# A two-layer decode kernel on one core: 1/std moved into the queries, output copies moved to ScalarE, the last weight loads cut differently

## The chip, the core and the metric

The kernel runs on one core of one Trainium2 chip. The metric is the device time of one execution in microseconds, given as the median of several runs. The core's engines run side by side, each in the order of its own instruction list: TensorE (PE, matmuls; PEld is its weight load), VectorE (DVE), ScalarE (ACT), GpSimd (POOL) and SyncE (SP, which here only issues transfers). Sixteen DMA engines bring data from the chip's memory; one `dma_start` is spread over all sixteen.

## The reference, cut to what matters

Four sequences (B = 4) are decoded by one token each. Width D = 640, 32 heads of DH = 128, a window of W = 1024 cached positions, FF = 1728. All is f32.

```python
x = A_x
for _ in range(2):
    n = layernorm(x)                          # (x - mean) / sqrt(var + 1e-5)
    q = n @ wq                                # per head: 4 x 128
    s = q . k[last 1024] * 128 ** -0.5        # per batch and head: 1024 scores
    x = x + (softmax(s) . v[last 1024]) @ wo
    x = x + relu(layernorm(x) @ w1) @ w2
```

Both rounds use the same weights and caches, so everything but what stays in the chip's SBUF is read twice.

## The kernel before, in words

**Data.** For each head the host packs one record of 128 rows x 9472 numbers (4736 KB): the head's columns of wq (`WQ`, 5 blocks of 128), keys (`K`, two halves of 4 batches x 512 positions), values (`V`, two halves) and its rows of wo (`WO`, 4 x 160). Records go in turn into five slots (`NS`) and a sixth, smaller buffer called `ring`. The last five heads of round 0 stay in their slots and are the first of round 1; head 26 (`SIXTH`) stays partly in `ring` and is next. w1 (5 blocks) and w2 (54 tiles of 128 x 160) of round 0 pass through `ring` in pieces (`MLP_RING`). In round 1, w1 goes into `ring`, w2 into one slot, cut into loads by `W2_SLOT`.

**Order of the loads.** `items` is the list of all loads, in order. `pump` issues the next load from SP as soon as no live data stands in its place; `done` says that a piece has been used and pumps again. A load also waits, on SP, until the semaphore that it is to count on is free. So one queue carries everything, in order, and what makes room for it is mostly TensorE's progress.

**Order of the work.** Each engine is wrapped in `InOrder`: what stands first in the code runs first on that engine. One turn of the loop over heads (line 442) puts down, for TensorE: the next head's scores, this head's values, the query of the head after the next (the first work on a newly landed record), `output_T` and `project`. VectorE in the same turn: `softmax`'s maximum (and its product with 1/std, line 347), `picks` (four operations), the copy of the new query into `qT` (line 329), the copy of the output into `oTs` (line 379), `weights` (seven operations). ScalarE: the exponential with its row sum.

**1/std.** `center` subtracts the mean from x, transposed in `xT`, and puts its squares' sums into `squares`; the division by the standard deviation is put off. `deviation` sums the squares over the partitions with a matmul into `o_ps[:, 8:12]`, one column for each batch, picks each partition's own batch with a mask (`of_batch` in attention, `pick` in the MLP; two VectorE operations), and takes the root on ScalarE into `rstd`, one number for each partition. `softmax` inverts it once per round and multiplies each head's maximum by it and, as the exponential's `scale`, the scores. In the MLP the ReLU takes it as its `scale`.

**The end.** After the last head, `center`, `mlp(1)`: 20 matmuls on w1 (the profile counts two for each f32 matmul), ReLU, two transposes, then 54 tiles of w2 in the order of their loads, adding into `acc`; VectorE copies `acc` and SP writes it out. `busy` is a matmul whose result nobody reads.

Of the kernel before, what the change touches and what calls it, by code (L numbers as in the profile page):

```python
# [32 lines left out]
F32 = mybir.dt.float32  # L33
AF = mybir.ActivationFunctionType
OP = mybir.AluOpType
AX = mybir.AxisListType
PSUM = bass.MemoryType.PSUM

P = 128
B, D, H, DH, W, FF = 4, 640, 32, 128, 1024, 1728  # L40
# [25 lines left out]

SIXTH_PIECES = [(3520, 5088), (5088, HELD), (0, 1600), (1600, 3520)]
W1_SLOT = [[0, 1], [2], [3], [4]]
W2_SLOT = [22, 20, 8, 4]
LATE = 5  # L70


# [22 lines left out]
def decode_kernel(ctx: ExitStack, tc: tile.TileContext, xf, rec, w1, w2, out):  # L95
    nc = tc.nc
    pe, dve, act, pool, sp = (InOrder(tc, e) for e in (nc.tensor, nc.vector, nc.scalar, nc.gpsimd, nc.sync))
    sb = ctx.enter_context(tc.tile_pool(name="sb", bufs=1))
# [11 lines left out]
    oTs = sb.tile([P, LATE, B], F32, name="oTs")  # L110
    qT = sb.tile([P, B], F32, name="qT")
    of_batch = sb.tile([P, B], F32, name="of_batch")
    of_block = sb.tile([P, 4], F32, name="of_block")
    pick = sb.tile([P, B], F32, name="pick")
    mrt = sb.tile([P, B], F32, name="mrt")
    small = sb.tile([P, 16], F32, name="small")
    nmax, rtot, rstd, eps, eps_dh, ones, unused, sums, tot0, tot1 = (small[:, i:i + 1] for i in range(10))
    squares, wq_mean, minus = small[:, 10:14], small[:, 14:15], small[:, 15:]
    tot = [tot0, tot1]
# [3 lines left out]
    sc_ps = [ps.tile([P, W], F32, name=f"sc_ps{i}") for i in range(2)]  # L123
    t_ps = ps.tile([P, 512], F32, name="t_ps")
    o_ps = ps.tile([P, 512], F32, name="o_ps")
# [33 lines left out]
    def home(h, r):  # L159

        if h == SIXTH:
            return "ring"
        return h % NS if not r or h >= LAST else (h + LAST) % NS
# [7 lines left out]
    def load(key, src, lo, hi, buf, col):  # L171
        items.append((key, src, lo, hi, buf, col))
# [14 lines left out]
    hs = order[0]  # L187
# [24 lines left out]
    n = 0  # L212
    for size in W2_SLOT:
        load(("w2", 1), w2, n * FD, (n + size) * FD, home(new[-5], 1), n * FD)
# [17 lines left out]
    def cols(key, lo, n):  # L232

        for x, y, buf, col in pieces(key):
            if x <= lo and lo + n <= y:
                return buffers[buf][:, col + lo - x:col + lo - x + n]
        raise KeyError((key, lo, n))
# [10 lines left out]
    def done(key, lo, hi):  # L248

        if key[0] == "rec" and key[1] == 0 and key[2] >= LAST:  # L250
            return
        if key == ("rec", 0, SIXTH):
            hi = min(hi, HELD)
        for x, y, buf, col in pieces(key):
            a, b = col + max(lo, x) - x, col + min(hi, y) - x
            if a < b:
                free(buf, a, b)
        pump()
# [18 lines left out]
    def busy(n, to=sc_ps[1]):  # L277

        pe.matmul(to[0:1, :n], ones, slot[home(LAST, 0)][:, K:K + n], start=True, stop=True)
# [30 lines left out]
        dve.tensor_tensor(spread[:, :KB * B].rearrange("p (k b) -> p k b", b=B), blocks, blocks, op=OP.mult)  # L310
        dve.tensor_reduce(squares, spread[:, :KB * B].rearrange("p (k b) -> p b k", b=B), op=OP.add, axis=AX.X)

    def deviation(rows, bias, scale):

        pe.matmul(o_ps[:, 8:8 + B], ones.to_broadcast([P, P]), squares, start=True, stop=True)
        dve.tensor_tensor(mrt, o_ps[:, 8:8 + B], rows, op=OP.mult)
        dve.tensor_reduce(sums, mrt, op=OP.add, axis=AX.X)
        act.activation(rstd, sums, AF.Sqrt, bias=bias, scale=scale / D)

    def xblock(k):  # L320
        return xT[:, 32 * k:32 * k + B]

    def query(r, h, s):
        q = sc_ps[s][:, :B]
        key = ("rec", r, h)
        for k in range(KB):
            pe.matmul(q, cols(key, WQ + k * DH, DH), xblock(k), start=(k == 0), stop=(k == KB - 1))
        done(key, WQ, K)
        dve.tensor_copy(qT, q)

    def scores(r, h, s, first=False):
        key = ("rec", r, h)
        for i in range(2):
            for b in range(B):
                pe.matmul(sc_ps[s][32 * b:32 * b + 4, 512 * i:512 * i + 512], qT[:, b:b + 1].to_broadcast([P, 4]),
                          cols(key, K + 512 * (B * i + b), 512), start=True, stop=True)
            done(key, K + VH * i, K + VH * i + VH)
            if first and i == 0:
                deviation(of_batch, eps_dh, float(DH))
                act.activation(unused, eps, AF.Exp)  # L340

    def softmax(s, first=False):

        dve.tensor_reduce(nmax, sc_ps[s], op=OP.max, axis=AX.X, negate=True)
        if first:
            dve.reciprocal(rstd, rstd)
        dve.tensor_tensor(nmax, nmax, rstd, op=OP.mult)
        act.activation(sc_ps[s], sc_ps[s], AF.Exp, bias=nmax, scale=rstd, accum_out=tot[s])

    def weights(s, parts=(0, 1)):  # L350
        if 0 in parts:
# [24 lines left out]

    def output_T(i, last=False):
        pe.matmul(o_ps[:, :B], on[last], pick, start=True, stop=True)
        dve.tensor_copy(oTs[:, i], o_ps[:, :B])

    def project(r, h, i, end):
        key = ("rec", r, h)
# [5 lines left out]
    def mlp(r):  # L388


        h_ps, front, back = sc_ps[0][:, :512], t_ps[:, :224], sc_ps[0][:, 512:768]
        for k in range(KB):
            for j in range(NB):
                pe.matmul(h_ps[32 * j:32 * j + B, :FQ], xblock(k), cols(("w1", r), k * FF + FQ * j, FQ),
                          start=(k == 0), stop=(k == KB - 1))
            done(("w1", r), k * FF, k * FF + FF)
            if k == 0:
                deviation(pick, eps, 1.0)
                dve.reciprocal(rstd, rstd)
            elif r == 0 and k < KB - 1:  # L400
                busy(512)
        act.activation(front, h_ps[:, :224], AF.Relu, scale=rstd)
        act.activation(back[:, :208], h_ps[:, 224:FQ], AF.Relu, scale=rstd)
        act.activation(back[:, 240:], h_ps[:, 416:FQ], AF.Relu, scale=rstd)
        dve.transpose(scratch[:, :224], front)
        dve.transpose(scratch[:, 224:], back)
        if r == 0:
            wq_means(LAST)
        else:
            busy(512)  # L410
        busy(256)
        key = ("w2", r)
        sizes = W2_SLOT if r else [size for name, size, _ in MLP_RING if name == "w2"]
        first = 0
        for i, size in enumerate(sizes):
            for s in range(first, first + size):
                m, n = TILES[s]
                w = cols(key, s * FD, FD)
                for part, q in ((m, n),) if m < 13 else ((13, n), (14, n + 2)):
                    pe.matmul(acc[32 * q:32 * q + B, :FD], hT[:, part, :B], w,  # L420
                              start=False, stop=(s >= len(TILES) - NB), skip_group_check=True)
            if r == 0 and i < len(sizes) - 2:
                busy(512)
            done(key, first * FD, (first + size) * FD)
            first += size
# [4 lines left out]
    for r in range(2):  # L430
        hs = order[r]
        late = LATE if r == 0 else 2
        if r == 0:
            center(fill=False)
            query(r, hs[0], 0)
        else:
            center(("rec", r, hs[0]))
        scores(r, hs[0], 0, True)
        softmax(0, True)
        query(r, hs[1], 1)  # L440
        weights(0)
        for n, h in enumerate(hs[:-2]):
            i = n - (H - late)
            s = (n + 1) % 2
            scores(r, hs[n + 1], s)
            softmax(s)
            values(r, h)
            picks(0)
            if n == H - 3:
                for _ in range(2):  # L450
                    busy(512)
            query(r, hs[n + 2], n % 2)
            output_T(max(i, 0))
            if i < 0:
                project(r, h, 0, False)
            weights(s, (0, 1) if n < H - 3 else (0,))
            if r == 0 and h == SIXTH:
                put_by()
            if r == 1 and hs[n + 2] == SIXTH:
                put_back()  # L460
        scores(r, hs[-1], 1)
        softmax(1)
        busy(512, sc_ps[0])
        weights(0, (1,))
        values(r, hs[-2], 0, (0, 1))
        weights(1)
        picks(0)
        values(r, hs[-1], 1, (1, 0))
        picks(1)
        dve.memset(sc_ps[0][:, 720:752], 0.0)  # L470
        output_T(late - 2)
        for i in range(late - 3):
            project(r, hs[H - late + i], i, False)
        if late == 2:
            project(r, hs[-2], 0, False)
        output_T(late - 1, True)
        for i in (late - 3, late - 1, late - 2) if late > 2 else (1,):
            project(r, hs[H - late + i], i, i == late - 2 or late == 2)
        center()
        mlp(r)  # L480
    dve.tensor_copy(x_sb, acc[:, :FD])
    sp.dma_start(out, x_sb)
# [38 lines left out]
```

## Time and profile before

| | |
|---|---|
| time, median of 3 runs | 714.68 us (714.43 to 715.10) |
| the profiled execution: its own time | 714.49 us |
| the profiled execution: span from first to last instruction | 712.8 us |
| granted TensorE clock, mean | 0.791 |
| busy: PE, DVE, ACT | 525.9 us (74%), 359.2 us (50%), 93.0 us (13%) |
| read from memory | 302.44 MB, 424 GB/s over the span |
| queue of the kernel's loads (q1) | 15264 packets, 99.1% of 16 engines' span |

The table is read from below: busy shares of the computing engines are means over the whole span, while the queue of the loads is at work nearly all of it. The queues q8 and q14 of the profile are the fetching of the engines' own instructions, by the same DMA engines. "Idle before" in a list of instructions is the time that an engine stood still just before one, with what ended it.

### The profile page before, as it was taken

The page shows a single profiled execution, that of the slowest core. Times are in us where ns is not written, and L with a number is a line of the kernel's source. Part 1 is how long each engine was busy: PE and PEld are TensorE (multiplying, and loading weights), DVE is VectorE, ACT ScalarE, POOL GpSimd, SP SyncE. Part 2 cuts the span into 40 slices and gives each one's busy share as a digit, 9 for nine tenths or more (in the row PEclk, how much of TensorE's full clock was granted, in tenths as well). Part 3 has the DMA queues.
Part 4 walks back from the last instruction along what each step waited for, and adds up shares of the span by engine and source line. Part 5 has one row for each costly group of instructions (what it writes and reads, how often), then busy time and mean ns, then how long its engine had stood idle before and what let it go on. Part 6 is the DMA issues. An engine that isn't in the chain of part 4 may idle for free.

```text
span 712.8 us, 8976 instructions
## 1 busy us (share of the span) xinstructions
PE 525.9 (74%) x3704; PEld 211.6 (30%) x3704; DVE 359.2 (50%) x1016; ACT 93.0 (13%) x145; POOL 1.1 (0%) x9
## 2 busy tenths in 40 slices
PE   4466877667676867778888898886777668777887
PEld 2132332313223232322324333332232323323323
DVE  3345445454444545445741787754644445445751
ACT  1201011010101011011111211201101010110201
POOL 0000000000000000000000000000000000000000
PEclk9987578786877676676999899877767775766997
DMA  9999999999999999999999999999999999999996
GB/s 375 442 435 428 427 439 437 428 426 442 435 422 434 439 435 421 432 441 420 425 412 395 427 434 428 445 427 436 433 436 428 435 432 430 432 437 420 430 423 287
DMA packets 15336, 303.10 MB, mean 425 GB/s; under 512 B 1712, under 2 KB 2112, under 8 KB 5312
## 3 DMA queue, kind: packets, MB, share of 16 engines
q1 hardware_dynamic: 15264, 302.52, 99.1%
q8 instruction: 29, 0.48, 0.2%
q14 instruction: 11, 0.09, 0.0%
q10 hardware_dynamic: 32, 0.01, 0.0%
HBM read 302.44 MB, written 0.08 MB: 424 GB/s over the span
## 4 chain that ended last, share of the span: by engine, by line
DMA 81%; PE 13%; DVE 4%; issue 1%; ACT 0%; another core or an unknown queue 0%; SPq 0%; DVEq 0%
DMA slot<-rec 69%; PE sc_ps L87 7%; DMA ring<-rec 6%; PE o_ps L87 3%; DMA ring<-w 3%; DMA slot<-w 3%; PE acc L87 3%; DVE scratch L87 2%; DVE small L87 1%; DVE oTs L87 1%; DVE t_ps L87 0%; ACT sc_ps L87 0%; DVE ring L87 0%; DVE mrt L87 0%
## 5 line engine op out<-in xcount | busy, mean ns | idle before, releaser
L87 PE MATMUL sc_ps<-xT,slot 128*128 128x4 f32 x620 | 100.5, 289 | 138.9 <-DMA slot<-rec 138.1
L87 PE MATMUL sc_ps<-slot,qT 128*4 128x512 f32 x992 | 195.0, 925 | 1.3 <-DVE qT L87 1.2
L87 PEld LDWEIGHTS sc_ps<-xT,slot 128*128 128x128 f32 x620 | 96.3, 240 | 194.4 <-issue 180.5
L87 ACT ACTIVATE sc_ps<-sc_ps,small 128x1024 f32<-128x1024 f32 (+1 forms) x68 | 76.6, 1127 | 551.1 <-DVE small L87 541.5
L87 PE MATMUL o_ps<-slot,scratch 128*16 128x512 f32 x960 | 137.1, 688 | 2.4 <-DVE scratch L87 1.8
L87 DVE TENSOR_REDUCE small<-sc_ps 128x1 f32<-128x1024 f32 x64 | 78.3, 1223 | 75.6 <-PE sc_ps L87 75.6
L87 DVE STREAM_TRANSPOSE t_ps<-sc_ps 128x512 f32<-128x512 f32 x128 | 93.2, 728 | 2.1
L87 DVE COPY qT<-sc_ps 128x4 f32<-128x4 f32 x63 | 10.1, 160 | 155.5 <-PE sc_ps L87 155.5
L87 PEld LDWEIGHTS o_ps<-slot,scratch 128*16 128x16 f32 x960 | 33.3, 121 | 131.4 <-issue 82.6
L87 DVE SCALAR_TENSOR_TENSOR scratch<-o_ps,of_block,scratch 128x128 f32<-128x128 f32 x186 | 65.2, 351 | 6.6
L87 PEld LDWEIGHTS sc_ps<-slot,qT 128*4 128x4 f32 x992 | 32.5, 113 | 80.2 <-issue 69.5
L87 PE MATMUL acc<-slot,oTs 128*4 128x160 f32 x496 | 36.8, 382 | 16.3 <-DVE oTs L87 15.8
L87 DVE TENSOR_SCALAR scratch<-o_ps,of_block 128x128 f32<-128x128 f32 x62 | 21.7, 350 | 37.2 <-PE o_ps L87 37.2
L87 PE MATMUL o_ps<-pick,scratch 128*128 128x4 f32 x128 | 29.4, 300 | 6.3 <-DVE scratch L87 6.1
L87 DVE TENSOR_TENSOR scratch<-t_ps,mrt 128x64 f32<-128x64 f32 x128 | 28.8, 225 | 4.7
L87 PEld LDWEIGHTS o_ps<-pick,scratch 128*128 128x128 f32 x128 | 26.2, 253 | 9.7 <-DVE scratch L87 8.9
L87 PE MATMUL sc_ps<-slot,small 128*1 128x512 f32 (+1 forms) x44 | 22.1, 599 | 2.9 <-DMA slot<-rec 2.4
L87 DVE COPY oTs<-o_ps 128x4 f32<-128x4 f32 x64 | 10.4, 162 | 15.5 <-PE o_ps L87 14.1
L87 DVE TENSOR_SCALAR mrt<-of_batch,small 128x4 f32<-128x4 f32 x64 | 14.7, 230 | 2.2
L87 DVE STREAM_TRANSPOSE scratch<-small 128x32 f32<-128x32 f32 x64 | 12.9, 202 | 2.4 <-ACT sc_ps L87 2.4
L87 PEld LDWEIGHTS acc<-slot,oTs 128*4 128x4 f32 x496 | 6.8, 84 | 22.1 <-DVE oTs L87 21.0
L87 PE MATMUL sc_ps<-ring,xT 128*4 128x432 f32 x80 | 10.3, 622 | 2.9 <-DMA ring<-w 2.6
(64 smaller groups left out, 118.5 us busy)
## 6 DMA issues: line engine op xcount, KB each, us to landing
slot<-rec SPq DMA_DIRECT2D x43, 4736.0 KB, 30.6
slot<-rec SPq DMA_DIRECT2D x17, 2368.0 KB, 17.1
slot<-rec SPq DMA_DIRECT2D x2, 4416.0 KB, 34.8
slot<-rec SPq DMA_DIRECT2D x7, 1024.0 KB, 9.0
ring<-w SPq DMA_DIRECT2D x8, 864.0 KB, 27.1
ring<-rec SPq DMA_DIRECT2D x1, 4576.0 KB, 40.1
slot<-rec SPq DMA_DIRECT2D x2, 2048.0 KB, 38.4
slot<-rec SPq DMA_DIRECT2D x3, 1344.0 KB
```

The source lines that it names most:

```text
L87: r = build(*args, **kwargs)
```

## The change

- `deviation` no longer picks each partition's batch before the root. The root of all four columns goes into a new tile `rstds` (128 x 4, each partition holds all four batches). The new function `row_rstd` inverts `rstds` and only then picks each partition's own number into `rstd` (three VectorE operations).
- `query` multiplies by `rstds` while it copies from PSUM to `qT`. The first head of each round is the exception: its query is copied (round 0) or corrected (round 1, in `center`) before 1/std is known, so its `softmax` does as before: `row_rstd`, the product of the maximum, `scale=rstd`. All other heads' `softmax` loses the product, and its exponential has `scale=1.0`.
- `output_T` copies the output with ScalarE (`AF.Copy`) instead of VectorE.
- The MLP calls `deviation` and `row_rstd(pick)`.
- `W2_SLOT`, the loads of w2 in round 1, becomes 22, 14, 10, 4 and 4 tiles instead of 22, 20, 8 and 4.

```diff
-W2_SLOT = [22, 20, 8, 4]
+W2_SLOT = [22, 14, 10, 4, 4]
...
+    rstds = sb.tile([P, B], F32, name="rstds")
...
-    def deviation(rows, bias, scale):
+    def deviation(bias, scale):
 
         pe.matmul(o_ps[:, 8:8 + B], ones.to_broadcast([P, P]), squares, start=True, stop=True)
-        dve.tensor_tensor(mrt, o_ps[:, 8:8 + B], rows, op=OP.mult)
-        dve.tensor_reduce(sums, mrt, op=OP.add, axis=AX.X)
-        act.activation(rstd, sums, AF.Sqrt, bias=bias, scale=scale / D)
+        act.activation(rstds, o_ps[:, 8:8 + B], AF.Sqrt, bias=bias, scale=scale / D)
+
+    def row_rstd(rows):
+
+        dve.reciprocal(rstds, rstds)
+        dve.tensor_tensor(mrt, rstds, rows, op=OP.mult)
+        dve.tensor_reduce(rstd, mrt, op=OP.add, axis=AX.X)
...
-    def query(r, h, s):
+    def query(r, h, s, first=False):
...
-        dve.tensor_copy(qT, q)
+        if first:
+            dve.tensor_copy(qT, q)
+        else:
+            dve.tensor_tensor(qT, q, rstds, op=OP.mult)
...
-                deviation(of_batch, eps_dh, float(DH))
+                deviation(eps_dh, float(DH))
...
         if first:
-            dve.reciprocal(rstd, rstd)
-        dve.tensor_tensor(nmax, nmax, rstd, op=OP.mult)
-        act.activation(sc_ps[s], sc_ps[s], AF.Exp, bias=nmax, scale=rstd, accum_out=tot[s])
+            row_rstd(of_batch)
+            dve.tensor_tensor(nmax, nmax, rstd, op=OP.mult)
+        act.activation(sc_ps[s], sc_ps[s], AF.Exp, bias=nmax, scale=rstd if first else 1.0, accum_out=tot[s])
...
-        dve.tensor_copy(oTs[:, i], o_ps[:, :B])
+        act.activation(oTs[:, i], o_ps[:, :B], AF.Copy)
...
-                deviation(pick, eps, 1.0)
-                dve.reciprocal(rstd, rstd)
+                deviation(eps, 1.0)
+                row_rstd(pick)
...
-            query(r, hs[0], 0)
+            query(r, hs[0], 0, True)
```

## The prediction, made before the changed kernel was run

> **What bounds the kernel now.** I read the page's DMA queues first, because they alone are near full.
>
> ```profile
> q1 hardware_dynamic: 15264, 302.52, 99.1%
> q8 instruction: 29, 0.48, 0.2%
> q14 instruction: 11, 0.09, 0.0%
> ```
>
> The columns are packets, MB and the share of 16 engines' span. The loads take 99.1%, and the change moves not a byte more or less. So only three things can move the end: what the slowest of the 16 DMA engines does beside the loads, gaps in the queue, and what follows the last landing. The chain of waits in order of time shows the landings (start us, length us, what):
>
> ```profile
> 197.92 30.86 DMA slot<-rec
> ...
> 232.63 30.74 DMA slot<-rec
> ...
> 510.25 31.24 DMA slot<-rec
> ...
> 545.34 30.54 DMA slot<-rec
> ...
> 578.26 31.12 DMA slot<-rec
> ...
> 613.13 29.75 DMA slot<-rec
> ...
> 683.10 23.86 DMA slot<-w
> 707.01 2.84 PE acc L87 x68
> ```
>
> Start plus length is a landing, complete only when the last of the 16 engines is done: 541.49, 575.88, 609.38, 642.88. Between them lie three records each, and the steps are 34.39, 33.50 and 33.50 us. The earlier pair, 228.78 and 263.37, is 34.59 apart. So some steps are 0.89 to 1.09 us too long. What stands in the long ones and not in the others? The DMA queues by narrow windows, in order at 43 to 44, 236.5 to 237, 559.1 to 559.8, 621.8 to 622.4 and 655.8 to 656.4 us, hold one small instruction packet each (11 packets of 0.09 MB in all: about 8 KB each):
>
> ```profile
> q14 instruction: 1, 0.01, 1.9%
> ...
> q14 instruction: 1, 0.01, 3.9%
> ...
> q14 instruction: 1, 0.01, 2.8%
> ...
> q14 instruction: 1, 0.01, 3.2%
> ...
> q14 instruction: 1, 0.01, 3.2%
> ```
>
> Eight of the eleven, of which the first, the third, the seventh and the last are shown here (all but the one at 622), come at a fixed count of VectorE instructions, as the busy table by stretches shows (x counts them):
>
> ```profile
> 0.00:43.30 43.30, 15.45 (x46) 0.96 0.97 413
> 43.30:655.80 612.50, 315.56 (x886) 0.77 1.00 430
> 655.80:712.80 57.00, 28.15 (x85) 0.86 0.90 383
> ```
>
> From the first fetch to the eighth are seven intervals, 886/7 = 126.6 instructions each. I read: VectorE's own instruction list is fetched in pieces, and the DMA engine that fetches it loses about a microsecond of its loads each time. That engine is then the last, and every landing waits for it. The end shows one engine alone (busy table, last columns DMA share and GB/s; then timelines of PE and PEld):
>
> ```profile
> 708.00:708.50 0.50, 0.50 (x20) 0.36 (x12) 0.00 (x0) 0.00 (x0) 0.00 (x0) 1.00 0.12 46
> 708.50:709.00 0.50, 0.50 (x22) 0.44 (x16) 0.00 (x0) 0.00 (x0) 0.00 (x0) 1.00 0.06 26
> ```
>
> ```profile
> 704.78 1.90 PE L87 MATMUL acc<-slot,scratch 128*4 128x160 f32 x44
> ```
>
> ```profile
> 708.56 0.45 PEld L87 LDWEIGHTS acc<-slot,scratch 128*4 128x4 f32 x16
> 709.35 0.11 PEld L87 LDWEIGHTS acc<-slot,scratch 128*4 128x4 f32 x8 [0.34 <-DMA slot<-w]
> ```
>
> A share of 0.06 is one engine of 16; 0.12 is two, or one and part of others. TensorE starts on the last four tiles at 709.35, released by the last load, and all that follows hangs on that.
>
> **The change part by part.** Costs are rows of the groups by form (count | busy us, mean ns):
>
> ```profile
> L87 DVE TENSOR_TENSOR small<-small 128x1 f32<-128x1 f32 x64 | 10.2, 159 | 2.2
> L87 DVE COPY oTs<-o_ps 128x4 f32<-128x4 f32 x64 | 10.4, 162 | 15.5 <-PE o_ps L87 14.1
> L87 DVE COPY qT<-sc_ps 128x4 f32<-128x4 f32 x63 | 10.1, 160 | 155.5 <-PE sc_ps L87 155.5
> L87 DVE TENSOR_TENSOR qT<-sc_ps,mrt 128x4 f32<-128x4 f32 x1 | 0.2, 161 | 0.2 <-PE sc_ps L87 0.2
> L87 ACT ACTIVATION_READ_ACCUMULATOR sc_ps<-sc_ps,small 128x1 f32 x64 | 12.2, 191 | 0.0
> L87 ACT ACTIVATE small<-small 128x1 f32<-128x1 f32 x6 | 1.6, 264 | 26.2 <-DVE small L87 26.2
> L87 DVE TENSOR_TENSOR mrt<-o_ps,of_batch 128x4 f32<-128x4 f32 x2 | 0.3, 163 | 3.5 <-PE o_ps L87 3.5
> L87 ACT ACTIVATE t_ps<-sc_ps,small 128x224 f32<-128x224 f32 x2 | 0.8, 422 | 8.0 <-PE sc_ps L87 8.0
> ```
>
> *Product in the query's copy.* The copy at 160 ns becomes a product at 161: nothing. *No product with the maximum* for 62 of 64 heads: 0.16 us less before each exponential. *Copies to ScalarE*: 64 x 0.162 us leave VectorE, with their wait for TensorE. No row has ScalarE copying four columns; the nearest lie at 0.191 and 0.264, and I take 0.25 (an ACTIVATE's, not the read-out's), so each copy is 0.03 to 0.10 us slower. In the turns where VectorE is never idle long this still shortens a head by up to 0.16 + 0.16 us and the wait; but the queue of the loads is full there, so it buys no time. Without that cover it would be worth some 0.5 us a head.
>
> *The end of round 1.* VectorE's copy stands behind `picks`, though TensorE has delivered long before:
>
> ```profile
> 692.25 0.39 PE L87 MATMUL o_ps<-pick,scratch 128*128 128x4 f32 x2
> ...
> 693.99 0.15 DVE L87 COPY oTs<-o_ps 128x4 f32<-128x4 f32 x1
> ...
> 695.01 0.16 DVE L87 COPY oTs<-o_ps 128x4 f32<-128x4 f32 x1 [0.86 <-PE o_ps L87]
> ...
> 696.01 0.33 DVE L87 TENSOR_REDUCE small<-acc 128x1 f32<-128x160 f32 x1 [0.84 <-PE acc L87]
> ```
>
> ScalarE can copy at about 692.7. The projection at 694.2 then goes ahead of the last `picks`, and the second copy, `center` (696.01) and ReLU come some 0.5 us earlier. The landing at 709.35 hides this too.
>
> *Root before the pick.* Two small VectorE operations (0.163 the row, the other alike) leave the path before the root and come back behind it; for the two first heads they now lie between maximum and exponential: +0.35 us, with gaps. Round 0's first is covered by the second record's landing. Round 1's is covered only by a full queue. In the MLPs ReLU waits for w1's matmuls (8.0 us idle, all ended by TensorE), not for this.
>
> *The loads of w2.* From 708.56 to 709.35 is 0.79 us for 4 tiles, from 707.01 to 708.56 1.55 us for 8: cutting costs 2 x 0.79 - 1.55 = 0.03 us a piece. Splitting helps TensorE start earlier, but TensorE already waits for the last piece. Ahead of it, TensorE's own work would not bind soon: 44 matmuls take 1.90 us, of which about 0.3 us is the last one's length (707.01 to 709.85 likewise ends one such length after its last start), so 0.037 each, and the 112 of all 54 tiles (two of them split) 4.5 us. Without waiting they would end at 709.3 from 704.78, at 708.8 with ReLU 0.5 us earlier, against 709.8 now.
>
> *The instruction lists.* VectorE loses 62 products and 64 copies: 46 + 886 + 85 = 1017 become 891 (the MLP and first-head parts cancel). Fetches stand at 46 + 126.6 k. For k = 6 that is 806, for k = 7 932, which is never reached: seven fetches, not eight. The slowest engine gets 0.89 to 1.09 us back. But the landing then falls to the next engine: one alone from somewhere in 708.0 to 708.5 until 709.0 is worth 0.5 to 0.75; I take 0.55, since 46 GB/s in the first half microsecond is nearly two engines' work (26 GB/s is one's).
>
> The sum: -0.55 + 0.03 = -0.52 us. The profiled execution took 714.49, its span 712.8; the median is 714.68, 0.19 above it. So the span becomes 712.3 and the median 714.16: **714.2 us**.
>
> **Rivals.**
>
> *Fetching costs nothing, or another engine fetches (0.26).* Then the full queue stays as it is: +0.03, **714.7**. For it: a step of 33.50 us (609.38 to 642.88) holds a q14 packet too, at 622 us, without being longer; I count that one to ScalarE's list, which another DMA engine may serve. Against it: the two long steps. The Trainium skill ("Runtime: NRT & Kernel Launch", section Instruction fetch mechanics) speaks for this rival: an engine fetches its list in blocks by its own DMA queue, and the cost of a block is "mostly hidden". By that rule the time stays at 714.7; the 34.39 us step of this trace says that on a full queue it does not hide.
>
> *More comes back (0.13).* The stretch of round 0's MLP is the one place where loads wait for room (busy table, DMA share and GB/s last; the third row is the full queue again):
>
> ```profile
> 372.00:376.00 4.00, 3.34 (x24) 0.42 (x19) 0.00 (x0) 0.00 (x0) 0.00 (x0) 1.00 0.95 360
> 384.00:388.00 4.00, 3.11 (x53) 1.65 (x45) 0.56 (x2) 0.00 (x0) 0.00 (x0) 1.00 1.01 367
> 392.00:396.00 4.00, 2.51 (x26) 0.84 (x29) 2.48 (x10) 1.96 (x4) 0.00 (x0) 1.00 1.02 426
> ```
>
> Against 426 GB/s these lose 4 x (1 - 360/426) = 0.62 and 0.55 us. An earlier slowest engine there frees pieces earlier; with half of the 1.17 and 0.9 instead of 0.55 the time is 714.68 - 0.9 - 0.58 + 0.03 = **713.2**. Against it: nothing in the change touches this stretch's matmuls.
>
> *Round 1 starts later (0.06).* The 0.35 us of the first exponential and 0.1 us for each copy of some eight heads delay the freeing of slots by up to 1.15 us. It decides only if the queue runs short after 388 us; the row at 392 says it does not. Price 0.35 to 1.15: **715.1 to 715.9**.
>
> *The fifth load of w2 ends by itself (0.05), the slower side.* The page lists a load that has the queue to itself:
>
> ```profile
> out<-scratch SPq DMA_DIRECT2D x1, 80.0 KB, 1.6
> ```
>
> That is 1.6 us from issue to landing for 80 KB, nearly all fixed. If the fifth load, which needs one more free semaphore, is issued only when the queue is empty, it costs 1.6 us at the very end: 714.68 + 1.6 = **716.3**. It decides if the issue comes after about 707 us; against it, the loads of w2 have their slot early: the chain has the second of them issued at 683.10. The Trainium skill ("DMA: Bandwidth & Descriptors", Anatomy of one DMA) gives a fixed 2.0 us for each DMA; were it paid in line, the sum would be 716.7. The 0.79 us between two landings says that it overlaps.
>
> **How the numbers follow.** Forecast 0.50, rivals 0.26, 0.13, 0.06, 0.05. A measurement of this kernel tells 0.2%, 1.43 us, from no change: 713.25 to 716.11. Of the "more" case nearly all lies below, with 0.02 from the forecast's edge: faster 0.15. The fifth-load case lies above: slower 0.05. The rest is within: 0.80. The range from 713.1 to 715.2 holds the forecast, the first rival, most of the second and the cheap end of the third.
>
> **What would show it.** In the new profile: about 891 VectorE instructions and one q14 packet fewer (or the same number, if ScalarE's longer list takes one more); steps of 33.5 us between landings except where VectorE's fetch falls, and three such fetches after 390 us instead of four; a last wait of TensorE for w2 near 708.8; `center` of round 1 near 695.5; SP issuing the fifth load before 700. I am wrong if the long steps stay where no fetch is, if the last landing is still at 709.3 with seven fetches, or if round 1's stretch after 388 us shows a DMA share under 1.

## The result, and the profile after

The changed kernel took **719.82 us** (median of 6 runs, 719.50 to 720.39) beside 715.31 us for the kernel before on the same chip. The ratio is **1.006**, 95% interval 1.0045 to 1.0075: slower by 0.6%, where 714.2 us was forecast with a range of 713.1 to 715.2. The profiled execution spans 717.7 us instead of 712.8.

The page's DMA queues after (packets, MB, share of 16 engines' span):

```profile
q1 hardware_dynamic: 15408, 302.52, 98.9%
q8 instruction: 29, 0.48, 0.3%
q14 instruction: 11, 0.09, 0.0%
```

The bytes are the same 302.52 MB, the 144 packets more are the fifth load of w2, and the queue is as full as before: 98.9% of a longer span. The queue did the same work in more time. The packets on q14 are eleven as before, not ten.

The chain of waits after (start us, length us, what):

```profile
119.52 31.61 DMA slot<-rec
...
153.52 31.30 DMA slot<-rec
...
187.20 31.30 DMA slot<-rec
...
222.37 29.81 DMA slot<-rec
...
492.22 30.33 DMA slot<-rec
...
526.41 29.82 DMA slot<-rec
...
696.51 17.78 DMA slot<-w
714.29 0.04 issue
714.34 0.50 PE acc L87 x8
```

Start plus length is a landing: 151.13, 184.82, 218.50 and 252.18, and later 522.55 and 556.23. Three records lie between neighbours, and each of these steps is 33.68 or 33.69 us. Before, the short steps were 33.50. So the loss isn't at one place: early and late in the run alike, a step is 0.18 us longer. The last load lands at 714.29, TensorE follows at once, and the end is as it was.

The busy table by stretches after (PE, PEld, DVE, ACT, POOL busy us with counts, then granted clock, DMA share, GB/s), cut at the first and the eighth fetch of VectorE, then round 1's start and the last half microseconds:

```profile
0.00:50.20 50.20, 25.43 (x130) 11.44 (x130) 17.20 (x48) 6.92 (x11) 1.13 (x9) 0.93 0.97 412
50.20:701.20 651.00, 487.19 (x3452) 194.52 (x3452) 321.54 (x839) 90.50 (x195) 0.00 (x0) 0.79 1.00 428
701.20:717.70 16.50, 7.45 (x132) 3.13 (x124) 1.19 (x3) 1.08 (x3) 0.00 (x0) 0.97 0.60 242
388.00:392.00 4.00, 3.18 (x44) 1.85 (x32) 1.40 (x7) 0.00 (x0) 0.00 (x0) 1.00 1.00 406
392.00:396.00 4.00, 4.00 (x24) 2.39 (x20) 1.76 (x5) 1.75 (x3) 0.00 (x0) 0.56 1.02 413
713.00:713.50 0.50, 0.50 (x20) 0.27 (x8) 0.00 (x0) 0.00 (x0) 0.00 (x0) 1.00 0.07 26
```

VectorE has 48 + 839 + 3 = 890 instructions, one from the 891 forecast. Yet an eighth fetch of its list came, with three of them left; the DMA queues at 701 to 701.6 us hold it:

```profile
q14 instruction: 1, 0.01, 3.4%
```

Round 1's start (the rows from 388 and 392 us) has a DMA share of 1.00 and 1.02, so the queue did not run short there. At 713.0 one DMA engine alone is still at work (0.07 of 16), as in the profile before.

The rows of the edits themselves, from the groups by form:

```profile
L87 ACT ACTIVATE sc_ps<-sc_ps,small 128x1024 f32<-128x1024 f32 x64 | 69.8, 1091 | 315.8 <-DVE small L87 315.8
L87 ACT ACTIVATE oTs<-o_ps 128x4 f32<-128x4 f32 x64 | 11.1, 174 | 246.0 <-PE o_ps L87 246.0
L87 DVE TENSOR_TENSOR qT<-sc_ps,rstds 128x4 f32<-128x4 f32 x62 | 9.9, 160 | 150.1 <-PE sc_ps L87 150.1
```

None of them has become dear, and the landings are what came later. So the lost time is looked for in the loads.

### The profile page after: what moved, and what is told of

Same layout as the page of the kernel before. It is cut to its first block, busy times and chain, and to the rows that moved or that the text cites. A ratio compares the mean times of both kernels' runs of the same rounds, so it can differ in the third digit from the quotient of the medians.

```text
span 717.7 us, 8921 instructions
## 1 busy us (share of the span) xinstructions
PE 520.1 (72%) x3704; PEld 209.1 (29%) x3704; DVE 339.9 (47%) x890; ACT 98.5 (14%) x209; POOL 1.1 (0%) x9
## 3 DMA queue, kind: packets, MB, share of 16 engines
q1 hardware_dynamic: 15408, 302.52, 98.9%
## 4 chain that ended last, share of the span: by engine, by line
DMA 73%; PE 21%; DVE 4%; ACT 1%; issue 1%; ACTq 0%; DVEq 0%
DMA slot<-rec 67%; PE sc_ps L87 12%; PE o_ps L87 6%; DMA ring<-w 3%; DVE scratch L87 3%; PE acc L87 3%; DMA slot<-w 2%; ACT oTs L87 1%; ACT sc_ps L87 0%; DVE small L87 0%; DVE t_ps L87 0%; ACTq L87 0%; ACT t_ps L87 0%; DVE xT L87 0%; DVE qT L87 0%
## 5 line engine op out<-in xcount | busy, mean ns | idle before, releaser
L87 PE MATMUL sc_ps<-slot,qT 128*4 128x512 f32 x992 | 198.5, 942 | 1.0 <-DVE qT L87 1.0
L87 PEld LDWEIGHTS sc_ps<-xT,slot 128*128 128x128 f32 x620 | 94.6, 236 | 201.1 <-DMA slot<-rec 183.7
L87 PE MATMUL o_ps<-slot,scratch 128*16 128x512 f32 x960 | 131.5, 665 | 0.9 <-DVE scratch L87 0.9
L87 ACT ACTIVATE sc_ps<-sc_ps,small 128x1024 f32<-128x1024 f32 (+1 forms) x68 | 71.1, 1046 | 315.9 <-DVE small L87 315.8
L87 DVE TENSOR_TENSOR qT<-sc_ps,rstds 128x4 f32<-128x4 f32 x62 | 9.9, 160 | 150.1 <-PE sc_ps L87 150.1
L87 ACT ACTIVATE oTs<-o_ps 128x4 f32<-128x4 f32 x64 | 11.1, 174 | 246.0 <-PE o_ps L87 246.0
L87 PE MATMUL sc_ps<-slot,small 128*1 128x512 f32 (+1 forms) x44 | 20.3, 553 | 0.6 <-DVE small L87 0.6
```

The costliest lines, as they stand in the source:

```text
L87: r = build(*args, **kwargs)
```

## The experiments

Each ratio is to the kernel before, run beside it on the same chip; an interval is at 95%.

### The chip, and the parts one by one

The kernel before again, without an edit:

> The kernel before, unchanged, profiled on the chip that runs the others. Theory A (this chip only moves data more slowly than the chip of the first profile: three records took 33.50 us there and 33.68 us in the changed kernel's profile): three records take 33.68 us here too, the ratio is 1.000, and the span is about 715. Theory B (the changed kernel itself slows the loads): 33.50 us between landings and a span of 712.8.

Measured: 714.78 us, ratio 0.9998 (0.9989 to 1.0006). So the chip isn't the cause. Three kernels take the change apart. The changed kernel with the old cut of w2:

```diff
-W2_SLOT = [22, 14, 10, 4, 4]
+W2_SLOT = [22, 20, 8, 4]
```

> The changed kernel with w2's last loads cut as before (22, 20, 8, 4). If the fifth load costs the time: ratio 1.000 to before. If it costs only its 0.03 us: the ratio of the changed kernel, 1.005 to 1.006, stays.

Measured: 719.83 us, 1.0065 (1.0052 to 1.0078). The loss stays whole. The kernel before with the new cut alone:

```diff
-W2_SLOT = [22, 20, 8, 4]
+W2_SLOT = [22, 14, 10, 4, 4]
```

> The kernel before with only the new cut of w2's loads (22, 14, 10, 4, 4). If the fifth load costs the time: ratio 1.005. If not: 1.000, with the last wait of TensorE for w2 later by 0.03 us at most.

Measured: 714.94 us, 0.9995 (0.9984 to 1.0006): the cut costs nothing that can be measured. The kernel before with ScalarE's copies alone:

```diff
-        dve.tensor_copy(oTs[:, i], o_ps[:, :B])
+        act.activation(oTs[:, i], o_ps[:, :B], AF.Copy)
```

> The kernel before with only the outputs' copies on ScalarE. The changed kernel's profile shows some 60 more semaphore waits on VectorE, in front of the first of the four picks. Theory C (the copies, through these waits or through ScalarE, cost the time): ratio 1.004 to 1.006. Theory D (the copies are hidden, the time is in the queries or the loads): 1.000.

Measured: 714.86 us, 1.0000 (0.9991 to 1.0009). What is left of the change is the work on 1/std, and with it a new tile.

### Where the loads land

`rstds` holds 16 bytes in each partition. The tiles of the pool `sb` lie one behind another, each from a multiple of 32 bytes, and `rstds` is declared ahead of the slots. In the memory plan of the two programs, slot 0 begins at byte 3072 of each partition before (12 x 256) and at 3104 after; all slots and `ring` move by those 32 bytes. Each load writes one row into each partition. Before, the rows of all loads but two (of 105) begin at a multiple of 256 bytes; after, every row begins 32 bytes further on. The packet records of the traces give the rows' times (ns; behind the start, four columns are medians by the bytes of a row, the mean is over all 5504 rows of 37888 bytes, the last is an instruction packet on q8, put down to TensorE because its list of 7497 entries makes 29 blocks of 256 and q8 has 29 packets of 16 KB):

```
start of slot 0        37888  18944  8192  2560   mean 37888   q8
before       3072       1401    705   309   102      1403.3    934
after        3104       1405    708   313   105      1408.6   1068
before + 32  3104       1405    708   313   104      1408.6   1073
before + 64  3136       1404    707   312   104      1407.6   1073
before +128  3200       1405    706   309   102      1407.1   1069
slots first   512       1401    705   309   102      1403.2    936
```

The last four lines are experiments below. At 32 bytes off, a row takes 2 to 4 ns more by the medians and 3 to 5 by the means, whether it has 2560 bytes (mean 102.5 to 105.3 ns) or 37888: a price for each row rather than for each byte. (At 128 the medians of the short rows stand still, but their means rise too: 102.5 to 105.0 ns for 2560 bytes.) The test is an unused tile in the kernel before, and no other edit:

```diff
+    pad = sb.tile([P, 8], F32, name="pad")
     slot = [sb.tile([P, REC], F32, name=f"slot{i}") for i in range(NS)]
```

> The kernel before with one edit: an unused tile of 32 bytes a row stands ahead of the slots, so that slots and ring start 32 bytes past a multiple of 256, as the new tile of 1/std makes them do in the changed kernel (slot 0 at byte 3104 instead of 3072). Theory E (the loads are slowed by where they land): ratio 1.006 to 1.007, three records in 33.68 us. Theory F (the work on 1/std slows the kernel): 1.000 and 33.50 us.

Measured: **719.58 us, 1.0064 (1.0051 to 1.0076)**. Thirty-two bytes that nobody uses make the whole loss. Its chain of waits:

```profile
120.82 30.47 DMA slot<-rec
...
154.09 30.89 DMA slot<-rec
...
188.84 29.83 DMA slot<-rec
```

Landings at 151.29, 184.98 and 218.67: steps of 33.69 us, those of the changed kernel. The counterpart is the changed kernel with `rstds` declared behind `ring`:

```diff
-    rstds = sb.tile([P, B], F32, name="rstds")
...
     ring = sb.tile([P, RING], F32, name="ring")
+    rstds = sb.tile([P, B], F32, name="rstds")
```

> The changed kernel with one edit: the tile of 1/std stands behind the ring, so slots and ring start where they did before. Theory E: ratio 0.999 to 1.000 and 33.50 us for three records. Theory F: 1.005 to 1.006 as in the changed kernel.

Measured: **714.83 us, 0.9996 (0.9986 to 1.0005)**. Its chain:

```profile
131.46 30.36 DMA slot<-rec
...
164.46 30.84 DMA slot<-rec
...
199.16 29.69 DMA slot<-rec
...
693.02 16.80 DMA slot<-w
```

The landings at 161.82, 195.30 and 228.85 are 33.48 and 33.55 apart, the kernel before's step; the last is at 709.82 instead of 714.29. The edit that only moves the buffers brings the loss, and the one that only moves them back takes it away. So the address is the cause, and the rest of the change costs nothing that can be measured. Three more runs ask how the address counts. The unused tile with 128 bytes (`[P, 32]`):

> The kernel before with slots and ring 128 bytes past a multiple of 256. If each row of a load that starts off a 256-byte line costs a little more whatever the distance: ratio 1.006. If only the odd 32 bytes count (starts off a 64- or 128-byte line): 1.000.

Measured: 718.57 us, 1.0053 (1.0040 to 1.0066). With 64 bytes (`[P, 16]`):

> The kernel before with an unused tile of 64 bytes ahead of the slots: slot 0 at byte 3136. Theory E with any start off a 256-byte line alike: 718.5 to 719.8, between the runs at 32 and at 128 bytes. If only the 32-byte start were bad and 64 a smaller line of its own: 714.8.

Measured: 718.96 us, 1.0051 (1.0039 to 1.0063). And `xT` and `scratch` declared behind `ring`, which moves slot 0 to byte 512 and `ring` to 189952, both multiples of 256:

> The kernel before with xT and scratch declared behind ring: slot 0 starts at byte 512 instead of 3072, ring at 189952 instead of 192512, all multiples of 256. Theory E (the start of a row against a 256-byte line decides): 714.8, within 0.3, rows of 37888 bytes at 1401 ns. Rival: any other place of the slots than the tuned one costs, or the order of the tiles: 718 to 720.

Measured: 715.28 us, 1.0002 (0.9988 to 1.0016). A quite different place is as good as the old one, as long as it is a multiple of 256; 32, 64 and 128 bytes off cost 0.5 to 0.6% alike.

The Trainium skill ("DMA: Bandwidth & Descriptors", section How a descriptor splits into AXI transactions) has a rule for it: a transaction starts on a 256-byte boundary, and a descriptor that doesn't start there is begun at the boundary below it, at the price of the extra beats of 32 bytes. The page tells this of what a transaction reads; here it is the place written to that moved. The sign agrees. The size does not follow the beats: by that count a row of 37888 bytes costs 1 beat more at 32 bytes off and 4 at 128, on 1184, which is an estimate of 1.2 and 4.7 ns; the means above rose by 5.3 and 3.8. What makes the price inside the DMA engine, these runs don't show.

### What a fetch of instructions costs

The prediction's only real gain was the eighth fetch of VectorE's list. Counted with its semaphore waits and the other entries that don't compute, the list is 1039 long before and 973 after, and fetches come when about 52, 180 and so on have begun, each some 128 later, so that the eighth is due at about 948; after the change it came at 964 of the 973. The 126 instructions saved are there, but 60 waits came in: the first of each four `picks` now waits for ScalarE's copy out of `o_ps`. The next two runs edit the aligned version, with `rstds` behind `ring`. The first takes the waits out by writing the output's transpose beside the sums in `acc`. What it leaves out is the true sum of the projections, which `acc` should hold, so only its time is read.

```diff
-        pe.matmul(o_ps[:, :B], on[last], pick, start=True, stop=True)
-        act.activation(oTs[:, i], o_ps[:, :B], AF.Copy)
+        pe.matmul(acc[:, 256:256 + B], on[last], pick, start=True, stop=True, skip_group_check=True)
+        act.activation(oTs[:, i], acc[:, 256:256 + B], AF.Copy)
```

> The changed kernel with the tile of 1/std behind the ring and the output's transpose put into unused columns of acc instead of o_ps, which takes away some 56 of the 60 extra semaphore waits on VectorE: its list is then 917 long instead of 973, under the 948 of the eighth fetch. The prediction's step (each fetch of VectorE's list costs the slowest DMA engine 0.9 to 1.1 us): seven fetches and 0.5 to 0.6 us less than e6, ratio 0.999. If fetches cost nothing: the same as e6.

Measured: 714.02 us, 0.9992 (0.9984 to 1.0001), with seven fetches. The median is 0.8 below the aligned version's, but the interval takes in both no change and the aligned version's 0.9996. The second run gets there with the computation whole: the transpose goes to `hold`, a buffer in PSUM that stands empty for 53 heads.

```diff
-            output_T(max(i, 0))
+            output_T(max(i, 0), to=hold[:, :B] if (n < 27 if r == 0 else n > 3) else o_ps[:, :B])
```

> The changed kernel with rstds behind ring (slots again at multiples of 256 bytes) and, while the buffer `hold` in PSUM stands empty (53 of the 64 heads), the output's transpose in `hold` instead of o_ps, so that VectorE's four picks need not wait for ScalarE's copy: VectorE's list with its waits falls from 973 to 921, under the 948 at which the eighth fetch came. Theory F (each fetch on the full queue costs the last landing 0.55 to 0.9 us, the prediction's only real gain): seven q14 packets of VectorE instead of eight, 714.83 of the aligned version minus 0.5 to 0.9, thus 713.9 to 714.3, and 0.5 to 0.9 below the kernel before beside it. Rival G (a fetch falls in slack that some other DMA engine gives back): within 0.2 of 714.8.

Measured: **714.48 us, 0.9990 (0.9982 to 0.9999)**, the best of the versions that compute the whole result, and below both kernels. It lies between the two expectations (713.9 to 714.3, and 714.6 to 715.0), and its interval overlaps the aligned version's: that the whole change now gains a little is shown, just; that the missing fetch makes the gain is not. The page's instruction queue and the end of the chain:

```profile
q14 instruction: 11, 0.08, 0.0%
```

```profile
692.38 16.47 DMA slot<-w
```

One of the eleven packets is of 48 bytes, at the start; ten of 8 KB remain, which are 0.08 MB and not 0.09. The last landing is at 708.85. Between the first and the last DMA engine's end of a load lie 3.6 us here in the last loads, 4.2 in the kernel before and 3.9 in the aligned version. By this lag the missing fetch is worth some 0.3 us. The third run goes the other way, in the kernel before:

```diff
+            for _ in range(5):
+                dve.memset(rtot, 0.0)
             dve.reciprocal(rtot, spread[:, 0:1])
```

> The kernel before with five tiny VectorE writes more for each head (a column of `small` set to 0, nobody reads it), 320 in all: VectorE's list with its waits grows from 1039 to 1359, past 1076, 1204 and 1332, so eleven fetches of VectorE instead of eight. The writes themselves lie in VectorE's idle time. Theory F (each fetch costs the end 0.55 to 0.9): 714.8 + 1.7 to 2.7 = 716.5 to 717.5. Rival G: 714.8, within 0.3. If the time grows but landings lengthen elsewhere than at the fetches, the writes' own time (0.3 us a head) is the cause and neither is shown.

Measured: **717.14 us, 1.0032 (1.0019 to 1.0044)**, some 2.3 us more. The page's instruction queue, the chain of waits, and the queues in two windows, at 492.6 to 493.2 and at 560.6 to 561.2 us:

```profile
q14 instruction: 14, 0.11, 0.0%
```

```profile
466.82 31.59 DMA slot<-rec
...
502.26 29.64 DMA slot<-rec
...
535.20 31.18 DMA slot<-rec
```

```profile
q14 instruction: 1, 0.01, 3.2%
...
q14 instruction: 1, 0.01, 3.2%
```

The landings are 498.41, 531.90 and 566.38. The step without a fetch in it is 33.49 us, that with the fetch at 560.9 is 34.48: 0.99 more. Load by load, by the semaphores that each DMA engine raises, and against the kernel before, the fastest DMA engine is level up to 369 us while the slowest is 0.8 behind (five fetches of VectorE by then, not four), and at the fetch of 694.9 us the slowest loses 0.9 more alone. So two of the three added fetches account for about 1.8 of the 2.5 us by which the last landing is later. The other 0.7 us arises between 377 and 392 us, where loads wait for room; whether the third fetch or the writes' own time makes it, these runs don't tell.

The Trainium skill ("Runtime: NRT & Kernel Launch", section Instruction fetch mechanics) calls the cost of crossing into the next block "mostly hidden". At the three places above it wasn't: 0.8 to 1.0 us.

But not every fetch of VectorE moves the landings. In the kernel before, the second one, at 142.1 us, falls between the landings of these two (the queues at 142 to 142.3 us stand below them):

```profile
97.91 30.31 DMA slot<-rec
...
132.08 29.64 DMA slot<-rec
```

```profile
q14 instruction: 1, 0.01, 6.4%
```

The landings are 128.22 and 161.72, so this step is 33.50 us with a fetch of VectorE in it, as short as those without. The lag between the first and the last engine stays at 2.2 to 2.3 us there, while it grows by 0.8 to 1.0 over the fetches at 236.6, 559.2 and 655.9. In the aligned version the eighth fetch, at 697.5 us, raises it from 3.7 to 4.0 only. A fetch without effect may have fallen to a DMA engine that wasn't the last; the packet records do not name the engine, so this isn't shown.

## Why the prediction was wrong

**What bounds the kernel: right.** The queue of the loads does, and the end follows the last landing. This held in every trace whose end is shown here, and the covers that the prediction named held too: with the buffers in place, the rest of the change shows no cost (0.9996).

**"The change moves not a byte more or less. So only three things can move the end": the step that failed.** It took the time of the full queue as fixed by its bytes. A fourth thing moves the end, the time of a row, and that hangs on where the row begins. The line `rstds = sb.tile(...)` stood in the diff; the prediction costed what is done with the tile, and not what lies behind it in memory. What it missed is +0.18 us on each 33.50 us. Adding the times of all rows and dividing by 16 engines gives 706.2 us before and 710.0 with the 32-byte tile, so 3.8 of the 4.9 us between these two medians of 714.68 and 719.58 (over all traces: 705.6 to 706.9 with the buffers at a multiple of 256, 709.3 to 710.8 off it). The slowest engine loses about 1 us more than the fastest (first to last engine 5.3 us in the last loads, against 4.2). The lengthened instruction packets in the table may be that, but at 64 and 128 bytes they are as long and the lag is 4.9 and 4.1; the packet records do not name the engine, and it stays open.

**The instruction lists: the mechanism holds, the count was wrong, and the price isn't the same at every fetch.** VectorE's instructions went to 890, against 891 forecast. The list that is fetched holds waits as well, which the busy table doesn't count, and moving the copies to another engine made 60 of them. The eighth fetch came nine entries before the list's end, and so the -0.55, the one gain in the sum, did not come. With the list at 921 and the slots in place, the ratio 0.9990 means -0.7 us (-1.3 to -0.1) for the whole change, against -0.52 forecast. That the sizes are near each other doesn't confirm the term: by the lag the fetch is worth some 0.3 us, and the prediction's reading that every landing waits for a fetch of VectorE overlooked the step of 33.50 us at 142.1. As for the rival that fetching costs nothing, its forecast of 714.7 is near what the aligned version shows (714.83), but for another reason: the fetch was still there.

**Product in the query's copy, no product with the maximum: right.** The copy's product is 160 ns, and nothing of it shows in the time. **Copies to ScalarE: right that they are hidden, 0.174 us instead of 0.25.** The row from which 0.191 was taken was the nearer one.

**The end of round 1: hidden, as said, but much larger.** In the aligned version's timeline of VectorE, `center` begins here:

```profile
693.24 0.33 DVE L87 TENSOR_REDUCE small<-acc 128x1 f32<-128x160 f32 x1 [1.06 <-PE acc L87]
```

That is 2.77 us before the 696.01 of the kernel before, though the last piece of the last record lands 0.2 us later (688.87 against 688.67, by the semaphores of the loads). The prediction had 0.5. Of the 2.77, 1.53 are there already at the last head's maximum on VectorE (683.48 against 685.01); the rest is TensorE's wait for the copy, in the kernel before and then in the aligned version:

```profile
694.20 0.46 PE L87 MATMUL acc<-slot,oTs 128*4 128x160 f32 x8 [1.56 <-DVE oTs L87]
...
691.05 0.46 PE L87 MATMUL acc<-slot,oTs 128*4 128x160 f32 x8 [0.32 <-ACT oTs L87]
```

The last load lands at 709.8 all the same.

**Root before the pick:** no run has it alone; with the rest, aligned, it costs nothing that can be measured. **The loads of w2: right.** The new cut alone is at 0.9995, and after the change the fifth load is issued at 696.51, long before the queue is empty.

**The other rivals.** *Round 1 starts later* and *the fifth load by itself* did not happen (shares of 1.00 and 1.02, issue at 696.51). *More comes back* needed the fetch to go. None of the rivals had the loads themselves slower, so no case reached 719.8, and the 0.05 on the slower side stood on a mechanism that wasn't the one.

**What was to show it.** Four of the marks set failed: the packets on q14 are eleven, not ten; VectorE's fetches after 390 us are four still (432.3, 511.3, 613.3 and 701.3), not three; TensorE's last wait for w2 ends at 714.3, not near 708.8; and the short steps are 33.68 us, not 33.5. The last of these is the mark that led to the cause.

## What to carry to other kernels

Where a full queue of loads sets the end, look up where each buffer that it fills begins before costing an edit: a new small tile ahead of the buffers moves them all, and off a multiple of 256 bytes the rows of the loads paid up to 5 ns each here, 0.5 to 0.6% of the time. Declare small tiles behind the large ones. And when work moves to another engine, count the waits that this adds to both lists: instructions that were saved on paper came back in part as waits, and with them the fetch.

## What the runs showed of the hardware

- When the rows of the loads begin 32, 64 or 128 bytes past a multiple of 256 in SBUF, a row of 37888 bytes takes 3.8 to 5.3 ns more in the mean and a row of 2560 bytes 2.5 to 2.9; the kernel's time is nearly the same for the three offsets (719.58, 718.96 and 718.57 us).
- With the loads off the multiple of 256, the instruction packets on q8 take 1068 to 1073 ns instead of 934 to 936; in the kernels with nothing but an unused tile more, the instructions are the same.
- ScalarE's exponential of 1024 columns takes 1091 ns where 62 of 64 have a constant scale, and 1177 with a scale for each partition, in the row of the kernel before:

```profile
L87 ACT ACTIVATE sc_ps<-sc_ps,small 128x1024 f32<-128x1024 f32 x64 | 75.3, 1177 | 551.0 <-DVE small L87 541.5 <-PE o_ps L87 9.2 <-DVE qT L87 0.3
```

- VectorE's and ScalarE's lists are fetched 8 KB at a time, about every 128 entries with the waits counted (VectorE's at 52, 183, 307 and so on in the kernel before, ScalarE's at 64 and 192); on the full queue some fetches moved the landings behind them by 0.8 to 1.0 us, others by nothing that shows.
